# Matmuls and transposes kept in the order of the text, and the second product of the states laid in by pairs

## The chip, the cores and the metric

One NeuronCore of a Trainium2 chip runs the whole program. The metric is device time in microseconds. Three runs of the kernel before took 641.52, 642.74 and 642.97 us; the median is 642.74 us.

## What is computed

Two layers in a row, all in float32. The first is a cross attention between tokens and states, the second a mixture of experts that sends each row to one expert.

```python
# x: (8 batches, 8 heads, 512 tokens, 64), state: (8, 8, 32, 64)
a  = softmax(x @ state.T / 8);  xread = a @ state        # 512 token rows of a batch
a2 = softmax(state @ x.T / 8);  sread = a2 @ x           # 32 state rows of a batch
x  = concat([xread, sread], axis=2) -> (8 * 544, 512)    # heads side by side
logits = x @ w_gate                                      # 8 experts
e = argmax(logits); g = softmax(logits)[e]
out = g * (relu(x @ w1[e]) @ w2[e])                      # w1: 512 x 1024, w2: 1024 x 512
```

## The kernel before, in words

**Attention.** For each batch `b` a generator `front(b)` transposes the tokens (`transpose_x`, L183, four groups of four 128x128 transposes into the PSUM tile `pt`, each group copied out by ACT before the next can use the one buffer that the tag "m" has), prepares the states (`prep_state`, L168: two transposes, two copies into `stT`, four small matmuls `pg`, copied to `gst`), and forms the scores `pc` (L189). The softmax over states and the one over tokens run on DVE, ACT and GpSimd. `back(b)` transposes the token softmax `a2` (L227), forms the state rows `pw` (L237), stores them to `st_dram`, and forms the tokens' logits `pl` (L254). The tag "s" (`pg`, `pw`, `pl`, `pr`) has one PSUM buffer too. `finish(b)` (L361) routes some batches: logits to one-hot rows on DVE (`route`), then counts per expert on PE (`pr`, L298).

**Tokens' experts.** In each batch the tokens are sent through one expert, that of most of the batch's tokens, whose number SP reads from `eb` before it loads the weights `w1t` and `w2t` (2 MB each, L323 and L327). `states_w1` forms `G` (`pG`, L408), `up` (L413) forms 8 tiles `hT` of two matmuls `ph` each, and `down` (L425) four tiles `py` of eight matmuls each, scaled and stored by ACT. `up` and `down` take an `insert` function, `piece`, which is called after every second of these 128x512 matmuls and there runs the next piece of other work.

**States' experts.** During the first `up` and the batches 0 and 1 that other work is the attention of batches 2 to 7. Then `logits_s` (L262) reads all state rows back (`srow`), the last batches are routed, and the rows are grouped by expert: `prs` (L492) ranks them, DVE works out slots, GpSimd scatters the rows to `ss_dram`, and SP reads groups of four times 32 rows back as `xg` (L552). From there the other work is `rounds()` (L623): four rounds of `round_x` (transposes `ptx`), four steps of the first product `round_up` (`pgh`, L581: 8 matmuls of 32 columns each, from two tiles `s1`), `round_h` (relu, eight transposes `pth`), and eight steps of the second product `round_down` (`pgy`, L599: four matmuls of 32 columns from a tile `s2`). Each matmul of a group of four goes to another quarter of PE's columns, with another expert's weights. A tile `s1` or `s2` is 1 MB in four transfers that SP issues; there are 4 buffers of `s1` and 3 of `s2`, and `fetch` orders the next tile when one has been used. A `yield` ends a piece: three per step of the first product, two per step of the second.

**What sets the order.** A scheduler puts the instructions of each engine in order, by its own picture of time; on PE it may set a later matmul ahead of an earlier one. SP, ACT, DVE and GpSimd each run their own list in its order.

```python
            for f in range(NFC):
                round_down(r, f)
                fetch(0, 1)
                yield
                yield
```

The line numbers are those of the kernel before.

Of the kernel before, what the change touches and what calls it, by code (L numbers as in the profile page):

```python
# [20 lines left out]
def kernel(  # L21
# [146 lines left out]
    def prep_state(b):  # L168
        pt = ps_m.tile([128, 2, 2, 2, NS], FP32, tag="m", name="pt")
        for g in range(2):  # L170
            nc.tensor.transpose(pt[:, g], st2[:, 2 * b + g], ident[:])
        for i in range(2):

            evict(stT[ts(i, 64), b].rearrange("p (g j) n -> p g j n", g=2)[:, :, :, ts(i, NS)],
                  pt[ts(i, 64), :, :, i, :])

        pg = ps_s.tile([128, 2, E], FP32, tag="s", name="pg")
        for j in range(NPR):
            nc.tensor.matmul(pg[ds(64 * (j % 2), 64), j // 2, :], lhsT=stT[:, b, j, :], rhs=wg[:, j, :],
                             start=True, stop=True, skip_group_check=True)  # L180
        evict(gst[:, b], pg[:])

    def transpose_x(b, xT, j):  # L183
        pt = ps_m.tile([128, NC, 128], FP32, tag="m", name="pt")
        for c in range(NC):
            nc.tensor.transpose(pt[:, c, :], x_nat[b][:, c, ts(j, 2), :], ident[:])  # L186
        nc.scalar.copy(xT[:, j], pt[:])  # L187

    def scores(b, xT):  # L189

        pc = ps_c.tile([128, 2, S], FP32, tag="c", name="pc")
        for j in range(NPR):
            nc.tensor.matmul(pc[ts(j % 2, 64), j // 2, :], lhsT=stT[:, b, j, :], rhs=xT[:, j],  # L193
                             start=True, stop=True, skip_group_check=True)
        return pc

# [30 lines left out]
    def transpose_write(a2):  # L227

        a2T = att.tile([128, 2, NC, 128], FP32, tag="a2T", name="a2T")
        for g in range(2):  # L230
            pt = ps_m.tile([128, NC, 128], FP32, tag="m", name="pt")
            for c in range(NC):
                nc.tensor.transpose(pt[:, c, :], a2[:, g, ts(c, 128)], ident[:])  # L233
            nc.scalar.copy(a2T[:, g], pt[:])  # L234
        return a2T

    def write_rows(b, a2T, s2):  # L237


        pw = ps_s.tile([128, 2, 2, D], FP32, tag="s", name="pw")  # L240
        for g in range(2):
            for c in range(NC):
                for i in range(2):
                    nc.tensor.matmul(pw[ts(i, 64), g], lhsT=a2T[:, g, c, ts(i, 64)],  # L244
                                     rhs=x_nat[b][:, c, ts(2 * g + i, 2), :],
                                     start=(c == 0), stop=(c == NC - 1), skip_group_check=True)
        xs = att.tile([128, 2, 2, D], FP32, tag="xs", name="xs")
        for g in range(2):
            nc.vector.tensor_scalar(xs[:, g], pw[:, g], s2[:, g:g + 1], None, ALU.mult)
        for i in range(4):  # L250
            nc.scalar.dma_start(out=st_dram[ts(b, NS)].rearrange("n (g i d) -> n g i d", g=2, i=4)[:, :, i, :],
                                in_=xs[ts(i, NS), :, i % 2, :])

    def logits_x(b):  # L254
        pl = ps_s.tile([128, NC, E], FP32, tag="s", name="pl")
        for c in range(NC):
            for g in range(2):
                nc.tensor.matmul(pl[:, c, :], lhsT=aT[:, b, g, ts(c, 128)], rhs=gst[:, b, g, :],  # L258
                                 start=(g == 0), stop=(g == 1), skip_group_check=True)
        evict(lg[:, ts(b, NC)], pl[:])  # L260

    def logits_s():  # L262
        sT = att.tile([128, NST, NDC, 128], FP32, tag="sT", bufs=1, name="sT")
        pl = ps_s.tile([128, NST, E], FP32, tag="s", name="pls")
        for t in range(NST):
            nc.sync.dma_start(out=srow[:, t, 0:DM], in_=st_dram[ts(t, 128)])
            pt = ps_m.tile([128, NDC, 128], FP32, tag="m", name="pt")
            for c in range(NDC):
                nc.tensor.transpose(pt[:, c, :], srow[:, t, ts(c, 128)], ident[:])
            evict(sT[:, t], pt[:])  # L270
        for t in range(NST):
            for c in range(NDC):
                nc.tensor.matmul(pl[:, t, :], lhsT=sT[:, t, c, :], rhs=wg[:, c, :],
                                 start=(c == 0), stop=(c == NDC - 1), skip_group_check=True)
        evict(lg[:, NX:], pl[:])

# [21 lines left out]
    def choose(b0, nb):  # L298

        pr = ps_s.tile([128, nb, E], FP32, tag="s", name="pr")  # L300
        ohb = oh[:, 0:NX].rearrange("p (b c) e -> p b c e", c=NC)
        for c in range(NC):
            nc.tensor.matmul(pr[:], lhsT=ones_b[:], rhs=ohb[:, ds(b0, nb), c, :],
                             start=(c == 0), stop=(c == NC - 1), skip_group_check=True)
# [95 lines left out]
    def states_w1(w1t, st):  # L400

        G = ffn.tile([128, 2, F], FP32, tag="G", bufs=1, name="G")
        for g in range(2):
            for k in range(2):
                pg = ps_h.tile([128, 512], FP32, tag="h", name="pG")
                for i in range(2):
                    j = 2 * g + i
                    nc.tensor.matmul(pg[ts(i, 64), :], lhsT=st[:, j, :], rhs=w1t[:, j, ts(k, 512)],  # L408
                                     start=True, stop=True, skip_group_check=True)
                evict(G[:, g, ts(k, 512)], pg[:])  # L410
        return G

    def up(G, a, insert=None):  # L413
        hT = [ffn.tile([128, S], FP32, tag="hT", bufs=NFC, name="hT") for _ in range(NFC)]
        for f in range(NFC):
            ph = ps_h.tile([128, S], FP32, tag="h", name="ph")
            for g in range(2):
                nc.tensor.matmul(ph[:], lhsT=G[:, g, ts(f, 128)], rhs=a[:, g, :],  # L418
                                 start=(g == 0), stop=(g == 1))
            relu(hT[f][:], ph[:])  # L420
            if insert:
# [70 lines left out]
    pr = ps_s.tile([128, NST + 1, E], FP32, tag="s", name="prs")  # L492
    for t in range(NST):
        for u in range(t):
            nc.tensor.matmul(pr[:, t, :], lhsT=ones_b[:], rhs=oh[:, NX + u, :],
                             start=(u == 0), stop=False, skip_group_check=True)
        nc.tensor.matmul(pr[:, t, :], lhsT=U128[:], rhs=oh[:, NX + t, :],
                         start=(t == 0), stop=True, skip_group_check=True)
    for u in range(NST):
        nc.tensor.matmul(pr[:, NST, :], lhsT=ones_b[:], rhs=oh[:, NX + u, :],  # L500
                         start=(u == 0), stop=(u == NST - 1), skip_group_check=True)
    ng_i = const.tile([128, E], I32)
    nc.vector.tensor_scalar(ng_i[:], pr[:, NST, :], 31.0, None, ALU.add)
# [65 lines left out]
    def round_x(r):  # L569
        pt = ps_t.tile([128, NDC, 128], FP32, tag="t", name="ptx")  # L570
        for c in range(NDC):
            nc.tensor.transpose(pt[:, c, :], rd[r]["xg"][:, ts(c, 128)], ident[:])
# [5 lines left out]
    def round_up(r, k):  # L578
        for half in range(2):
            for q in range(4):  # L580
                nc.tensor.matmul(rd[r]["ph"][half][ts(q, 32), :], lhsT=rd[r]["xT"][:, k, ts(q, 32)],  # L581
                                 rhs=rd[r][1, k, half][:, q, :], start=(k == 0), stop=(k == NDC - 1),
                                 skip_group_check=True)

    def round_h(r):
# [4 lines left out]
        for u in range(2):  # L590
            pt = ps_t.tile([128, 4, 128], FP32, tag="t", name="pth")
            for i in range(4):
                nc.tensor.transpose(pt[:, i, :], h[:, ts(4 * u + i, 128)], ident[:])  # L593
            evict(hT[:, ts(u, 4)], pt[:])
        rd[r].update(hT=hT, py=ps_g.tile([128, DM], FP32, tag="g", bufs=2, name="pgy"))

    def round_down(r, f):
        for q in range(4):
            nc.tensor.matmul(rd[r]["py"][ts(q, 32), :], lhsT=rd[r]["hT"][:, f, ts(q, 32)],  # L599
                             rhs=rd[r][2, f][:, q, :], start=(f == 0), stop=(f == NFC - 1),  # L600
                             skip_group_check=True)

# [20 lines left out]
    def rounds():  # L623
# [3 lines left out]
        for r in range(NR):  # L627
# [128 lines left out]
```

## Time and profile before

| what | value |
|---|---|
| median of three runs | 642.74 us |
| the profiled execution's own time | 642.71 us |
| its span on the core | 640.8 us |
| PE busy | 600.3 us, 94% of the span |
| DVE, ACT, GpSimd busy | 131.6, 108.9, 23.4 us |
| moved by DMA | 123.15 MB, 192 GB/s over the span |
| `py` and `ph` matmuls, busy | 241.8 and 123.3 us |
| `pgh` and `pgy` matmuls, busy | 60.3 and 59.5 us |

A float32 matmul stands in the trace as two rows, one per pass, so `py` with its 256 matmuls has 512 rows. "x4" in a timeline is four such rows. The busy time of PE counts a stretch once where rows overlap. The idle time before a row, with what ended it, stands in brackets.

### The profile page before, as it was taken

What the parts mean: (1) busy time and instruction counts of PE and PEld (TensorE: products, weight loads), DVE (VectorE), ACT (ScalarE), POOL (GpSimd) and SP (SyncE); (2) the same over time, 40 slices, a digit from 0 to 9 for tenths busy, and PEclk for the clock granted to TensorE, in tenths of its full rate; (3) what the DMA queues carried; (4) which work ended last, traced back from release to release, by engine and by line L of the source; (5) the groups of instructions that cost most, each with busy time, mean ns of one, the idle gap of its engine ahead of it and who ended that gap; (6) DMA issues with size and microseconds to landing.
All of it is one profiled execution on the core that took longest, in us unless ns stands there. A gap on an engine that the chain in (4) does not pass through costs nothing.

```text
span 640.8 us, 6269 instructions
## 1 busy us (share of the span) xinstructions
PE 600.3 (94%) x2225; PEld 235.7 (37%) x2225; DVE 131.6 (21%) x287; ACT 108.9 (17%) x202; POOL 23.4 (4%) x29
## 2 busy tenths in 40 slices
PE   1778699999999999799999999999999999999997
PEld 0355334555455544123223242332322322333343
DVE  1335521544643414000110011000110001000100
ACT  1332311323413212001111010100111001111100
POOL 1011010101101101000000000000000000000000
PEclk9996799999999999999999999999999999999999
DMA  9433930376131044976985879677697779635501
GB/s 242 86 70 79 383 134 1 102 234 186 31 137 37 20 167 133 297 258 198 348 324 164 298 258 316 227 266 262 228 360 249 263 241 313 212 133 165 197 17 50
DMA packets 96497, 123.15 MB, mean 192 GB/s; under 512 B 45775, under 2 KB 45775, under 8 KB 96464
## 3 DMA queue, kind: packets, MB, share of 16 engines
q1 hardware_dynamic: 83552, 110.65, 52.8%
q10 hardware_dynamic: 12432, 11.04, 5.2%
q0 software_dynamic: 480, 1.05, 0.4%
q8 instruction: 18, 0.29, 0.2%
q14 instruction: 15, 0.12, 0.1%
HBM read 111.69 MB, written 11.54 MB: 192 GB/s over the span
## 4 chain that ended last, share of the span: by engine, by line
PE 85%; issue 6%; ACT 4%; DMA 3%; DVE 2%; ACTq 1%; SPq 0%; POOL 0%; POOLq 0%
PE py L429 33%; PE ph L418 16%; PE pgh L581 9%; PE pgy L599 8%; PE pG L408 4%; PE pc L193 4%; PE pt L186 3%; PE pw L244 2%; PE pl L258 2%; PE pt L233 1%; DMA st<-in_state_dram 1%; ACT xT L187 1%; DMA ss_dram<-srow,slot_i 1%; ACT a L221 1%; PE pth L593 1%
## 5 line engine op out<-in xcount | busy, mean ns | idle before, releaser
L429 PE MATMUL py<-w2t,hT 128*128 128x512 f32 x512 | 241.8, 606 | 0.0
L429 PEld LDWEIGHTS py<-w2t,hT 128*128 128x128 f32 x512 | 89.9, 190 | 129.4 <-issue 128.3
L418 PE MATMUL ph<-aT,G 128*128 128x512 f32 x256 | 123.3, 609 | 0.0
L418 PEld LDWEIGHTS ph<-aT,G 128*128 128x128 f32 x256 | 44.3, 189 | 66.0 <-issue 64.1
L581 PE MATMUL pgh<-s,sxT 128*32 128x512 f32 x256 | 60.3, 602 | 0.0
L442 ACT ACTIVATE y<-py,gw 128x512 f32<-128x512 f32 x32 | 22.0, 687 | 224.2 <-PE py L429 200.6
L599 PE MATMUL pgy<-s,shT 128*32 128x512 f32 x256 | 59.5, 604 | 0.0
L398 DVE TENSOR_SCALAR hT<-ph 128x512 f32<-128x512 f32 x31 | 21.4, 691 | 173.1 <-PE ph L418 173.1
L186 PE MATMUL pt<-ident,x_nat 128*128 128x128 f32 x128 | 26.3, 333 | 20.7 <-ACT xT L187 12.1
L396 ACT ACTIVATE hT<-ph 128x512 f32<-128x512 f32 x33 | 19.7, 596 | 129.4 <-PE ph L418 126.0
L408 PE MATMUL pG<-w1t,stT 128*64 128x512 f32 x128 | 34.7, 613 | 0.0
L186 PEld LDWEIGHTS pt<-ident,x_nat 128*128 128x128 f32 x128 | 18.0, 167 | 37.8 <-ACT xT L187 15.9
L193 PE MATMUL pc<-xT,stT 128*64 128x512 f32 x64 | 28.5, 773 | 0.0
L187 ACT COPY xT<-pt 128x512 f32<-128x512 f32 x32 | 18.7, 585 | 40.8 <-PE pt L186 40.8
L581 PEld LDWEIGHTS pgh<-s,sxT 128*32 128x32 f32 x256 | 9.4, 108 | 42.0 <-issue 32.8
L210 POOL TENSOR_TENSOR sx<-sx,sm 128x1024 f32<-128x1024 f32 x8 | 15.3, 1912 | 200.1 <-DVE sm L209 119.1
L599 PEld LDWEIGHTS pgy<-s,shT 128*32 128x32 f32 x256 | 8.6, 108 | 37.7 <-issue 33.1
L244 PE MATMUL pw<-x_nat,a2T 128*64 128x128 f32 x256 | 19.9, 304 | 0.0
L244 PEld LDWEIGHTS pw<-x_nat,a2T 128*64 128x64 f32 x256 | 17.1, 153 | 4.9 <-issue 4.4
L258 PEld LDWEIGHTS pl<-gst,aT 128*128 128x128 f32 x128 | 15.2, 194 | 5.8 <-issue 5.3
L607 POOL DMA_INDIRECT out_dram<-ys,xg x4 | 3.9, 977 | 361.7 <-DMA s<-in_moe_w_dram 202.0
L233 PE MATMUL pt<-ident,a 128*128 128x128 f32 x64 | 12.0, 319 | 4.2 <-ACT a2T L234 2.0
(117 smaller groups left out, 251.7 us busy)
## 6 DMA issues: line engine op xcount, KB each, us to landing
s<-in_moe_w_dram SPq DMA_DIRECT2D x256, 256.0 KB, 5.1
w1t<-in_moe_w_dram SPq DMA_DIRECT2D x8, 2048.0 KB, 8.0
w2t<-in_moe_w_dram SPq DMA_DIRECT2D x8, 2048.0 KB, 12.4
x_nat<-in_x_dram SPq DMA_DIRECT2D x32, 256.0 KB, 3.8
out_dram<-y ACTq DMA_DIRECT2D x32, 256.0 KB, 4.2
ss_dram<-blank ACTq DMA_DIRECT2D x4, 257.0 KB, 7.8
xg<-ss_dram SPq DMA_DIRECT2D x4, 257.0 KB
st<-in_state_dram ACTq DMA_DIRECT2D x2, 448.0 KB, 9.0
```

Source lines behind the costliest of these rows:

```text
L186: nc.tensor.transpose(pt[:, c, :], x_nat[b][:, c, ts(j, 2), :], ident[:])
L187: nc.scalar.copy(xT[:, j], pt[:])
L193: nc.tensor.matmul(pc[ts(j % 2, 64), j // 2, :], lhsT=stT[:, b, j, :], rhs=xT[:, j], start=True, stop=True, skip_group_check=True)
L244: nc.tensor.matmul(pw[ts(i, 64), g], lhsT=a2T[:, g, c, ts(i, 64)], rhs=x_nat[b][:, c, ts(2 * g + i, 2), :], start=(c == 0), stop=(c == NC ...
L258: nc.tensor.matmul(pl[:, c, :], lhsT=aT[:, b, g, ts(c, 128)], rhs=gst[:, b, g, :], start=(g == 0), stop=(g == 1), skip_group_check=True)
L398: nc.vector.tensor_scalar(dst, src, 0.0, None, ALU.max)
L408: nc.tensor.matmul(pg[ts(i, 64), :], lhsT=st[:, j, :], rhs=w1t[:, j, ts(k, 512)], start=True, stop=True, skip_group_check=True)
L418: nc.tensor.matmul(ph[:], lhsT=G[:, g, ts(f, 128)], rhs=a[:, g, :], start=(g == 0), stop=(g == 1))
L429: nc.tensor.matmul(py[:], lhsT=hT[f][:, ts(c, 128)], rhs=w2t[:, f, :], start=(f == 0), stop=(f == NFC - 1))
L442: nc.scalar.activation(y[:], py[:], AF.Copy, scale=gw[:, NC * b + c, :])
L581: nc.tensor.matmul(rd[r]["ph"][half][ts(q, 32), :], lhsT=rd[r]["xT"][:, k, ts(q, 32)], rhs=rd[r][1, k, half][:, q, :], start=(k == 0), sto ...
L599: nc.tensor.matmul(rd[r]["py"][ts(q, 32), :], lhsT=rd[r]["hT"][:, f, ts(q, 32)], rhs=rd[r][2, f][:, q, :], start=(f == 0), stop=(f == NFC ...
```

## The change

Every matmul and every transpose now goes through `mm` or `tp`, which tell the scheduler to leave PE's instructions in the order in which the text issues them. The second product of the states is laid in by two steps at a time: two steps, then four yields, in place of one step and two yields, twice.

```diff
+    def mm(*args, **kw):
+
+        tc.keep_in_program_order(nc.tensor.matmul(*args, **kw))
+
+    def tp(*args):
+        tc.keep_in_program_order(nc.tensor.transpose(*args))
+
...
-            nc.tensor.transpose(pt[:, g], st2[:, 2 * b + g], ident[:])
+            tp(pt[:, g], st2[:, 2 * b + g], ident[:])
...
-                nc.tensor.matmul(py[:], lhsT=hT[f][:, ts(c, 128)], rhs=w2t[:, f, :],
+                mm(py[:], lhsT=hT[f][:, ts(c, 128)], rhs=w2t[:, f, :],
...
-            for f in range(NFC):
-                round_down(r, f)
-                fetch(0, 1)
+            for f in range(0, NFC, 2):
+                for i in range(2):
+                    round_down(r, f + i)
+                    fetch(0, 1)
+                yield
+                yield
                 yield
                 yield
```

All other matmuls and transposes of the program are changed as the two shown. No instruction is added or taken away.

The rounds, on PE. `pgh` is the states' first product and `pgy` their second; the number in `s_1613` tells the weight tile. Before, near the start of round 0:

```order
L429 MATMUL py<-w2t,hT 128x512 x11
L572 MATMUL ptx<-ident,xg 128x128 x4
L429 MATMUL py<-w2t,hT 128x512
L581 MATMUL pgh<-s_1613,sxT 32x512 x2
L429 MATMUL py<-w2t,hT 128x512
L581 MATMUL pgh<-s_1613,sxT 32x512
L429 MATMUL py<-w2t,hT 128x512
L581 MATMUL pgh<-s_1613,sxT 32x512
L429 MATMUL py<-w2t,hT 128x512
L581 MATMUL pgh<-s_1618,sxT 32x512 x2
L429 MATMUL py<-w2t,hT 128x512
L581 MATMUL pgh<-s_1618,sxT 32x512
```

and now:

```order
L124 MATMUL py<-w2t,hT 128x512 x2
L127 MATMUL ptx<-ident,xg 128x128 x4
L124 MATMUL py<-w2t,hT 128x512 x4
L124 MATMUL pgh<-s_1613,sxT 32x512 x4
L124 MATMUL pgh<-s_1618,sxT 32x512 x4
L124 MATMUL py<-w2t,hT 128x512 x6
L124 MATMUL pgh<-s_1623,sxT 32x512 x4
L124 MATMUL pgh<-s_1628,sxT 32x512 x4
```

The eight matmuls of a step stand together, and from the first `ptx` on all 256 matmuls of 32 columns stand in 32 groups of eight, where before they stood in 101 groups of one to eleven. Nine `py` that stood ahead of the first `ptx` now stand behind it.

The end of routing, on PE: `srow` are state rows read back, `pls` their logits, `pr` the counts, `prs` the ranks. Before:

```order
L418 MATMUL ph<-aT,G 128x512 x2
L269 MATMUL pt<-ident,srow 128x128 x4
L418 MATMUL ph<-aT,G 128x512
L273 MATMUL pls<-wg,sT 128x8 x4
L418 MATMUL ph<-aT,G 128x512 x7
L269 MATMUL pt<-ident,srow 128x128 x4
L418 MATMUL ph<-aT,G 128x512
L273 MATMUL pls<-wg,sT 128x8 x4
L418 MATMUL ph<-aT,G 128x512 x3
L303 LDWEIGHTS ones_b
L303 MATMUL pr<-oh,ones_b 128x24
```

and now:

```order
L124 MATMUL ph<-aT,G 128x512 x2
L127 MATMUL pt<-ident,srow 128x128 x8
L124 MATMUL pls<-wg,sT 128x8 x8
L124 LDWEIGHTS ones_b
L124 MATMUL pr<-oh,ones_b 128x24
```

Both sets of row transposes, all of `pls` and `pr` now stand in one piece behind two of the `ph`; the other fourteen `ph` come behind `pr`, and `prs` behind those.

The attention of batches 3 and 2 inside `down`, on PE. `a_692` is the token softmax of one batch. Before:

```order
L186 MATMUL pt<-ident,x_nat 128x128 x4
L429 MATMUL py<-w2t,hT 128x512
L233 MATMUL pt<-ident,a_692 128x128 x4
L429 MATMUL py<-w2t,hT 128x512
L233 MATMUL pt<-ident,a_692 128x128 x4
L429 MATMUL py<-w2t,hT 128x512
L171 MATMUL pt<-ident,st_130 128x128 x2
L429 MATMUL py<-w2t,hT 128x512
L179 MATMUL pg<-wg,stT 64x8 x4
L193 MATMUL pc<-xT,stT 64x512
L244 MATMUL pw<-x_nat,a2T 64x128 x16
```

and now:

```order
L127 MATMUL pt<-ident,x_nat 128x128 x4
L127 MATMUL pt<-ident,a_692 128x128 x8
L124 MATMUL py<-w2t,hT 128x512 x2
L127 MATMUL pt<-ident,st_130 128x128 x2
L124 MATMUL pg<-wg,stT 64x8 x4
L124 MATMUL pw<-x_nat,a2T 64x128 x16
L124 MATMUL py<-w2t,hT 128x512 x2
L124 MATMUL pc<-xT,stT 64x512 x4
```

Groups that share one PSUM buffer, between which a `py` stood before, now stand next to each other. The same holds for five batches. Ahead of all this, the scheduler had set the token transposes and scores of batches 2 and 3 before the first `pG`; they now stand behind it, inside `up` and `down`.

## Rows read from the trace of the kernel before

**Rows 1.** The page, part 1: busy time, share and instructions of each engine.

```profile
PE 600.3 (94%) x2225; PEld 235.7 (37%) x2225; DVE 131.6 (21%) x287; ACT 108.9 (17%) x202; POOL 23.4 (4%) x29
```

**Rows 2.** PE timeline, second round: start, duration (us), line, tiles, rows merged.

```profile
330.84 1.05 PE L599 MATMUL pgy<-s,shT 128*32 128x512 f32 x4
331.82 1.12 PE L429 MATMUL py<-w2t,hT 128*128 128x512 f32 x2
332.88 1.04 PE L599 MATMUL pgy<-s,shT 128*32 128x512 f32 x2
```

**Rows 3.** PE timeline, last round and the end.

```profile
556.68 1.92 PE L581 MATMUL pgh<-s,sxT 128*32 128x512 f32 x16
558.53 5.42 PE L429 MATMUL py<-w2t,hT 128*128 128x512 f32 x12
563.88 1.93 PE L581 MATMUL pgh<-s,sxT 128*32 128x512 f32 x16
...
614.46 22.58 PE L429 MATMUL py<-w2t,hT 128*128 128x512 f32 x52
```

**Rows 4.** PE timeline, first and last visit to the 32-column matmuls.

```profile
262.85 1.67 PE L581 MATMUL pgh<-s,sxT 128*32 128x512 f32 x4
...
613.47 1.07 PE L599 MATMUL pgy<-s,shT 128*32 128x512 f32 x8
```

**Rows 5.** PE timeline, from the end of routing to the first round.

```profile
226.32 1.88 PE L418 MATMUL ph<-aT,G 128*128 128x512 f32 x4
...
237.68 0.63 PE L269 MATMUL pt<-ident,srow 128*128 128x128 f32 x4 [1.09 <-DMA srow<-st_dram]
...
239.00 1.04 PE L273 MATMUL pls<-wg,sT 128*128 128x8 f32 x8
...
242.55 0.25 PE L303 MATMUL pr<-oh,ones_b 128*128 128x24 bf16 x4
...
244.53 0.19 PE L500 MATMUL prs<-oh,ones_b 128*128 128x8 bf16 x2
...
261.44 0.63 PE L572 MATMUL ptx<-ident,xg 128*128 128x128 f32 x4 [3.33 <-DMA s<-in_moe_w_dram]
```

**Rows 6.** Timeline of SP's issues, the same stretch.

```profile
227.55 0.35 SPq L266 DMA_DIRECT2D srow<-st_dram  x1
...
258.22 0.34 SPq L552 DMA_DIRECT2D xg<-ss_dram  x1
259.10 11.13 SPq L558 DMA_DIRECT2D s<-in_moe_w_dram  x16
270.62 11.84 SPq L565 DMA_DIRECT2D s<-in_moe_w_dram  x12
```

**Rows 7.** PE timeline, attention: groups that wait for a copy, and one that doesn't.

```profile
71.20 0.66 PE L186 MATMUL pt<-ident,x_nat 128*128 128x128 f32 x4 [0.68 <-ACT xT L187]
...
78.83 0.60 PE L179 MATMUL pg<-wg,stT 128*64 128x8 f32 x8 [0.67 <-ACT stT L128]
...
126.00 0.60 PE L186 MATMUL pt<-ident,x_nat 128*128 128x128 f32 x4
126.43 1.02 PE L429 MATMUL py<-w2t,hT 128*128 128x512 f32 x2
```

**Rows 8.** SP's issue of the first weights.

```profile
61.96 0.39 SPq L325 DMA_DIRECT2D w1t<-in_moe_w_dram  x1
```

**Rows 9.** The view of the tile `w1t`: its eight loads.

```profile
DMA to landing us min/median/max: 7.7/8.0/10.4
```

**Rows 10.** PE timeline, the first `up`.

```profile
86.17 14.00 PE L418 MATMUL ph<-aT,G 128*128 128x512 f32 x32
```

**Rows 11.** Stretches: busy time by engine, PEclk (granted clock), DMA share, GB/s.

```profile
48.00:52.00 4.00, 2.59 (x10) 1.80 (x11) 3.58 (x11) 1.30 (x3) 0.00 (x0) 0.51 0.02 4
...
261.40:637.10 375.70, 374.11 (x1146) 117.01 (x1146) 29.29 (x42) 37.54 (x61) 3.91 (x4) 1.00 0.70 237
460.00:480.00 20.00, 20.00 (x62) 5.88 (x54) 2.77 (x4) 2.36 (x4) 0.00 (x0) 1.00 0.96 325
```

More of the change, by code (lines that the diff above doesn't have):

```diff
@@ L178, in prep_state @@
         for j in range(NPR):
-            nc.tensor.matmul(pg[ds(64 * (j % 2), 64), j // 2, :], lhsT=stT[:, b, j, :], rhs=wg[:, j, :],
+            mm(pg[ds(64 * (j % 2), 64), j // 2, :], lhsT=stT[:, b, j, :], rhs=wg[:, j, :],
                              start=True, stop=True, skip_group_check=True)
@@ L185, in transpose_x @@
         for c in range(NC):
-            nc.tensor.transpose(pt[:, c, :], x_nat[b][:, c, ts(j, 2), :], ident[:])
+            tp(pt[:, c, :], x_nat[b][:, c, ts(j, 2), :], ident[:])
         nc.scalar.copy(xT[:, j], pt[:])
@@ L192, in scores @@
         for j in range(NPR):
-            nc.tensor.matmul(pc[ts(j % 2, 64), j // 2, :], lhsT=stT[:, b, j, :], rhs=xT[:, j],
+            mm(pc[ts(j % 2, 64), j // 2, :], lhsT=stT[:, b, j, :], rhs=xT[:, j],
                              start=True, stop=True, skip_group_check=True)
@@ L243, in write_rows @@
                 for i in range(2):
-                    nc.tensor.matmul(pw[ts(i, 64), g], lhsT=a2T[:, g, c, ts(i, 64)],
+                    mm(pw[ts(i, 64), g], lhsT=a2T[:, g, c, ts(i, 64)],
                                      rhs=x_nat[b][:, c, ts(2 * g + i, 2), :],
@@ L257, in logits_x @@
             for g in range(2):
-                nc.tensor.matmul(pl[:, c, :], lhsT=aT[:, b, g, ts(c, 128)], rhs=gst[:, b, g, :],
+                mm(pl[:, c, :], lhsT=aT[:, b, g, ts(c, 128)], rhs=gst[:, b, g, :],
                                  start=(g == 0), stop=(g == 1), skip_group_check=True)
@@ L268, in logits_s @@
             for c in range(NDC):
-                nc.tensor.transpose(pt[:, c, :], srow[:, t, ts(c, 128)], ident[:])
+                tp(pt[:, c, :], srow[:, t, ts(c, 128)], ident[:])
             evict(sT[:, t], pt[:])
@@ L272, in logits_s @@
             for c in range(NDC):
-                nc.tensor.matmul(pl[:, t, :], lhsT=sT[:, t, c, :], rhs=wg[:, c, :],
+                mm(pl[:, t, :], lhsT=sT[:, t, c, :], rhs=wg[:, c, :],
                                  start=(c == 0), stop=(c == NDC - 1), skip_group_check=True)
@@ L302, in choose @@
         for c in range(NC):
-            nc.tensor.matmul(pr[:], lhsT=ones_b[:], rhs=ohb[:, ds(b0, nb), c, :],
+            mm(pr[:], lhsT=ones_b[:], rhs=ohb[:, ds(b0, nb), c, :],
                              start=(c == 0), stop=(c == NC - 1), skip_group_check=True)
@@ L407, in states_w1 @@
                     j = 2 * g + i
-                    nc.tensor.matmul(pg[ts(i, 64), :], lhsT=st[:, j, :], rhs=w1t[:, j, ts(k, 512)],
+                    mm(pg[ts(i, 64), :], lhsT=st[:, j, :], rhs=w1t[:, j, ts(k, 512)],
                                      start=True, stop=True, skip_group_check=True)
@@ L417, in up @@
             for g in range(2):
-                nc.tensor.matmul(ph[:], lhsT=G[:, g, ts(f, 128)], rhs=a[:, g, :],
+                mm(ph[:], lhsT=G[:, g, ts(f, 128)], rhs=a[:, g, :],
                                  start=(g == 0), stop=(g == 1))
@@ L494 @@
         for u in range(t):
-            nc.tensor.matmul(pr[:, t, :], lhsT=ones_b[:], rhs=oh[:, NX + u, :],
+            mm(pr[:, t, :], lhsT=ones_b[:], rhs=oh[:, NX + u, :],
                              start=(u == 0), stop=False, skip_group_check=True)
-        nc.tensor.matmul(pr[:, t, :], lhsT=U128[:], rhs=oh[:, NX + t, :],
+        mm(pr[:, t, :], lhsT=U128[:], rhs=oh[:, NX + t, :],
                          start=(t == 0), stop=True, skip_group_check=True)
     for u in range(NST):
-        nc.tensor.matmul(pr[:, NST, :], lhsT=ones_b[:], rhs=oh[:, NX + u, :],
+        mm(pr[:, NST, :], lhsT=ones_b[:], rhs=oh[:, NX + u, :],
                          start=(u == 0), stop=(u == NST - 1), skip_group_check=True)
@@ L580, in round_up @@
             for q in range(4):
-                nc.tensor.matmul(rd[r]["ph"][half][ts(q, 32), :], lhsT=rd[r]["xT"][:, k, ts(q, 32)],
+                mm(rd[r]["ph"][half][ts(q, 32), :], lhsT=rd[r]["xT"][:, k, ts(q, 32)],
                                  rhs=rd[r][1, k, half][:, q, :], start=(k == 0), stop=(k == NDC - 1),
@@ L598, in round_down @@
         for q in range(4):
-            nc.tensor.matmul(rd[r]["py"][ts(q, 32), :], lhsT=rd[r]["hT"][:, f, ts(q, 32)],
+            mm(rd[r]["py"][ts(q, 32), :], lhsT=rd[r]["hT"][:, f, ts(q, 32)],
                              rhs=rd[r][2, f][:, q, :], start=(f == 0), stop=(f == NFC - 1),
```

6 lines of the change are left out of this document (3 added, 3 removed).

## The prediction

> **What bounds the kernel now.** I read the busy times first. PE is busy for 600.3 of 640.8 us and no other engine for a quarter of that [rows 1], so the question is what PE's time is made of. Then I read PE's timeline in the rounds. A visit to the 32-column matmuls takes 0.98 us from its start to the next row's (330.84 to 331.82), whether it holds four rows or two: the one `py` behind it starts at 331.82, and the visit at 332.88 holds one matmul [rows 2]. That `py` takes 1.06 us (331.82 to 332.88), while in an unbroken run two rows take 0.87 us (22.58 us for 52 rows) [rows 3]. In the last round, where the same matmuls happen to stand in the order of the text, sixteen rows take 1.85 us (556.68 to 558.53), and the six `py` behind them 5.35 us (558.53 to 563.88) [rows 3]. So a group of four matmuls on four quarters of the columns costs as little as one alone, about 0.9 us, and each change between narrow and full matmuls costs some tenths. The reader is to see that PE's 94% hides matmuls that ran alone where four could have run together. Third, the places at which PE waits, since an order that may not be left turns waits into idle time: the end of routing [rows 5, 6], the attention [rows 7] and the first weights [rows 8 to 10].
>
> **The change part by part.** The sum is made against the profiled execution: 642.71 us, of which the span is 640.8, practically the median of 642.74.
>
> *1. The rounds, a gain.* Before, PE makes 101 visits to the 32-column matmuls; the first starts at 262.85, the last at 613.47 [rows 4]. From start to start of the next row they add up to 110.2 us. The new order has 32 visits of eight matmuls, at 1.85 us each [rows 3] 59.2 us: 51.0 us less. Behind a visit the first full matmuls pay 0.2 us (5.35 against 12 rows at 0.434, which is 5.21, gives 0.14; 1.06 against 0.87 gives 0.19); 69 visits fewer are 13 us less at 0.19. Against this, nine `py` that ran before the first `ptx` now come behind it: 9 x 0.87 = 7.8 us. The eight `pth` of a round now stand together though they share one PSUM buffer; each such pair of groups waits for the copy, some 0.9 us as worked out under 4, four times, 3.6 us, of which before paid about half: +2. Sum from the first `ptx` to the end of PE's work: -51 - 13 + 8 + 2 = **-54**. Bounds: if the visits cost 1.0 per four as in rows 2, 32 x 2.0 = 64, and -49; if nothing is paid for `pth`, -56.
>
> *2. The start of the rounds, a loss.* At `ptx` (261.44) SP has only begun: 16 transfers of `s1`, issued from 259.10 on for 11.13 us, then 12 of `s2` from 270.62 for 11.84 us [rows 6]. In the text's order step 3 of the first product comes about 19 us behind `ptx` (four `py` 3.5, then two visits of 1.85 and two runs of 5.35, and about 1 for the second tile). Its two tiles are transfers 29 to 36, queued on SP behind the other 28, which end at 282.46, 21 us behind `ptx`; eight more at the 0.7 us of the first sixteen are 5.6 us. That is 26.6, and PE would wait 7 or 8 us. It is less if the queue runs better without the pauses of the second group, so I take **+6**, from 0 to 12.
>
> *3. The end of routing, a loss.* Take as zero the end of batch 1's `down`, just before the `ph` at 226.32 [rows 5]. The second `srow` is issued right after, at 227.55 [rows 6], behind a 2 MB weight load, and is there at 237.68, 11.4 us on [rows 5]. Before, PE fills this with `ph`; now it has two of them, 1.7 us, and waits. From the transposes at 237.68 to `pr` at 242.55 are 4.9 us, which the text's order has to wait through too, and the other four `pls` (1.04 us at 239.00 [rows 5]) come in front: `pr` at 17.3. Then fourteen `ph` at 0.87, 12.2 us, part of them at the lower clock after such a wait (+2.5): `prs` at 32. From `prs` (244.53) to `ptx` (261.44) were 16.9 us [rows 5], through DVE, the scatter and `xg` (258.22 [rows 6]); PE has only the `pG` and two `py` for it. So `ptx` at 48.9, against 35.1 before: **+13.8**. Bounds: without the clock's part and with `pr` at once +10; +17 if the copies in between queue.
>
> *4. The attention, a loss.* Where two groups share a PSUM buffer, PE idles 0.68 us behind its 0.66 us of transposes [rows 7], 1.34 us where a group followed by a `py` takes 0.43 (126.00 to 126.43) [rows 7]: 0.9 us each. `pg` behind the state transposes idles 0.67 us the same way [rows 7]. In the new order each of five batches has four such neighbours (last token transposes and first `a2` transposes, the two halves of `a2`, state transposes and `pg`, `pg` and `pw`, which share the tag "s"), and two more stand alone: 22 waits, at 0.85 us **+18.7**. Bounds: 22 x 0.67 = 15; 25 if DVE or ACT are busy when the copy comes.
>
> *5. The front.* The token work of batches 2 and 3 no longer stands in front of the first `pG`. The first weights are issued at 61.96 [rows 8], once `pw` of batch 1 has let the fifth `x` load go. In the new order three groups of transposes leave the way to that `pw`, a `pr` enters it; I take 3 us earlier, 59, and 7.7 for landing [rows 9]: 66.7. Four pairs of `pG`, half of them at the lower clock, take some 6 us, so `up` starts near 73 in place of 86.17 [rows 10], -13. The moved work then costs, at the full clock, eight groups of token transposes at 0.43 (3.5), two of `a2` (0.9), states (1.2), and eight score matmuls, two side by side (16 rows x 0.217 + 2 x 0.2 = 3.9): +9.5. Sum **-3.5**, from -6 to +2 (weights not earlier at all, 61.96 + 8).
>
> *6. Transfers during the rounds.* The stretch from 261.4 on moved 237 GB/s over 375.7 us [rows 11], 89 MB. With part 1 the last visit ends some 295 us behind `ptx`, part 2 makes it 301: 296 GB/s have to flow. 20 us at 325 are in the trace [rows 11], so it can, but pairs of `s2` tiles out of three buffers have little slack. I take **+3**, from 0 to 20.
>
> The copies on ACT and DVE, the stores, GpSimd and DVE's softmax cost nothing: PE's matmuls cover them, as those engines are busy for a fifth of the span or less [rows 1].
>
> Sum: -54 + 6 + 13.8 + 18.7 - 3.5 + 3 = -16. 642.7 - 16 = 626.7, in round numbers **627 us**.
>
> **The rivals.**
>
> *The clock falls in the attention.* From 48 to 52 us the granted clock is 0.51, the lower of the two levels, 1.2 GHz [rows 11]; in that part of the program PE does transposes with waits between them, as at 71.20 [rows 7]. If each of the five batches of part 4 drops to that level for 10 us, the matmuls in it take 5 us more: 25 us, 652 us, slower. It turns the sign from 6.5 us of low clock per batch on. Against it: the stretch from 261.4 on keeps 1.00 [rows 11] although it comes right behind a wait of 3.33 us [rows 5], and part 4's waits are 0.7 us between full matmuls. The Trainium skill speaks for it, "TensorE: Matmul & The Clock Gate", section "HAM oscillation — how this bites in real kernels": bursts of matmuls with waits between them run throttled, every one of them. By that rule the time would be this rival's; the rows at 48 us bear it out, those behind 261.44 do not. Chance 0.08.
>
> *The transfers become the bound.* If the rounds' 89 MB flow at 265 GB/s, they take 336 us, 35 more than the 301, and the time is 627 - 3 + 35 = 659; at 280 it is 318 us and 641. So from 278 down the change is no gain. For it: each tile waits for a buffer, and two are now wanted at once. Against: the 325 over 20 us, with PE the slower side [rows 11]. Middle value 642; chance 0.12.
>
> *The waits of parts 2 to 4 are smaller.* If the start of the rounds costs 0, routing +10 and the attention +15, the time is 642.7 - 54 + 10 + 15 - 3.5 + 3 = 613. For it: what a wait delays is partly waited for again later (parts 2 and 3 overlap, as DMA goes on). Chance 0.17.
>
> **How the numbers follow.** The forecast, 627, has 0.63; its own range, from the bounds, is 615 to 639. The whole range has to leave out no more than 0.2: 606 takes in the third case, and 645 the better half of the transfers' case; the clock's case is left out. A measurement tells about 0.2%, 1.3 us, from no change. Faster by more: 0.61 of the forecast, all 0.17 of the third case and little of the transfers' case: 0.80. Same: 0.05. Slower: the clock, half of the transfers' case and a rest: 0.15.
>
> **What would show it.** Part 1 is right if the rounds show only visits of sixteen rows at 1.85 us, and the stretch from `ptx` to PE's end is near 327 us (375.6 before); wrong if 32-column rows wait for `s`. Part 2: a wait of several us at the third step of round 0. Part 3: PE idle for about 9 us before the second `srow` transposes and 11 before the first `ptx`. Part 4: idle time of 0.6 to 0.9 us in front of `a2` transposes, `pg` and `pw`, with the granted clock at 1.00 there. Part 5: the first `ph` near 73. The forecast falls if transfers hold PE in every round, or if the clock is low between 80 and 230 us.

## The result and the profile after

The changed kernel takes 625.38 us (median of 4 runs, 624.16 to 626.47) against 642.86 for the kernel before on the same chip: a ratio of 0.9728, with a 95% interval of 0.9701 to 0.9755. The forecast was 627. The profiled execution took 626.47 us, of which the span is 624.6; before it was 642.71 and 640.8, so the two profiles are 16.2 us apart.

The profiled execution of one experiment below (the text's order in the rounds alone) was disturbed, so that kernel was run once more for its profile.

The page's busy line of the kernel after, beside [rows 1]:

```profile
PE 541.8 (87%) x2225; PEld 241.4 (39%) x2225; DVE 132.1 (21%) x287; ACT 109.3 (17%) x202; POOL 23.4 (4%) x29
```

PE makes the same 2225 matmuls in 58.5 us less, but its share falls from 94% to 87%: the span fell by 16 us only, and the rest became idle time. The page's groups of the 32-column matmuls, first of the kernel after, then of before (tiles, count, busy us, mean ns, idle time before them):

```profile
L124 PE MATMUL pgh<-s,sxT 128*32 128x512 f32 x256 | 35.4, 620 | 6.7 <-DMA s<-in_moe_w_dram 6.7
L124 PE MATMUL pgy<-s,shT 128*32 128x512 f32 x256 | 31.7, 599 | 0.0
```

```profile
L581 PE MATMUL pgh<-s,sxT 128*32 128x512 f32 x256 | 60.3, 602 | 0.0
L599 PE MATMUL pgy<-s,shT 128*32 128x512 f32 x256 | 59.5, 604 | 0.0
```

The mean time of one is the same, about 0.6 us; what fell is their joint busy time, from 119.8 to 67.1 us, since four now run side by side. The reader sees here why a mean says nothing of matmuls that overlap.

PE's timeline of the kernel after at the stretch ends that the prediction used (start, duration, idle time before it):

```profile
72.83 1.98 PE L124 MATMUL ph<-aT,G 128*128 128x512 f32 x4
...
236.00 1.88 PE L124 MATMUL ph<-aT,G 128*128 128x512 f32 x4
...
247.34 1.09 PE L127 MATMUL pt<-ident,srow 128*128 128x128 f32 x4 [9.03 <-DMA srow<-st_dram]
...
253.51 0.28 PE L124 MATMUL pr<-oh,ones_b 128*128 128x24 bf16 x4 [1.86 <-DVE oh L297]
253.63 14.64 PE L124 MATMUL ph<-aT,G 128*128 128x512 f32 x28
...
283.62 1.09 PE L127 MATMUL ptx<-ident,xg 128*128 128x128 f32 x4 [9.43 <-DMA s<-in_moe_w_dram]
284.50 5.91 PE L124 MATMUL py<-w2t,hT 128*128 128x512 f32 x8
...
297.67 1.92 PE L124 MATMUL pgh<-s,sxT 128*32 128x512 f32 x16
299.52 5.42 PE L124 MATMUL py<-w2t,hT 128*128 128x512 f32 x12
311.62 6.46 PE L124 MATMUL pgh<-s,sxT 128*32 128x512 f32 x16 [6.68 <-DMA s<-in_moe_w_dram]
...
594.81 26.02 PE L124 MATMUL py<-w2t,hT 128*128 128x512 f32 x60
```

With the starts in [rows 3, 5, 10], and the end of PE's work at 594.81 + 26.02 = 620.83 (before 614.46 + 22.58 = 637.04), the difference falls into four stretches:

| stretch on PE | before, us | after, us | difference | forecast (parts) |
|---|---|---|---|---|
| to the first `ph` | 86.17 | 72.83 | -13.3 | -13 (5) |
| first `ph` to the end of batch 1's `down` | 140.15 | 163.17 | +23.0 | +28.2 (4, rest of 5) |
| from there to the first `ptx` | 35.12 | 47.62 | +12.5 | +13.8 (3) |
| first `ptx` to the end of PE's work | 375.60 | 337.21 | -38.4 | -45 (1, 2, 6) |
| sum | 637.04 | 620.83 | -16.2 | -16 |

The second stretch is the attention. PE's timeline of the kernel after in one batch, beside [rows 7]:

```profile
100.74 0.60 PE L127 MATMUL pt<-ident,x_nat 128*128 128x128 f32 x4
102.02 0.66 PE L127 MATMUL pt<-ident,a 128*128 128x128 f32 x4 [0.68 <-ACT xT L194]
103.35 0.66 PE L127 MATMUL pt<-ident,a 128*128 128x128 f32 x4 [0.68 <-ACT a2T L241]
103.84 1.88 PE L124 MATMUL py<-w2t,hT 128*128 128x512 f32 x4
105.56 0.38 PE L127 MATMUL pt<-ident,st 128*128 128x128 f32 x2
106.61 0.41 PE L124 MATMUL pg<-wg,stT 128*64 128x8 f32 x8 [0.67 <-ACT stT L135]
107.29 1.97 PE L124 MATMUL pw<-x_nat,a2T 128*64 128x128 f32 x32 [0.28 <-DVE gst L137]
```

All four forecast neighbours wait, three by 0.67 or 0.68 us and the last by 0.28. And the stretches of the kernel after, columns as in [rows 11]:

```profile
80.00:241.00 161.00, 143.89 (x755) 76.76 (x754) 66.82 (x132) 47.93 (x97) 11.47 (x6) 1.00 0.27 83
241.00:260.00 19.00, 10.80 (x34) 7.16 (x35) 3.58 (x20) 1.48 (x3) 0.00 (x0) 0.55 0.25 97
318.00:480.00 162.00, 160.54 (x593) 60.09 (x596) 17.41 (x25) 20.39 (x33) 1.96 (x2) 1.00 0.92 318
```

The clock stays at 1.00 through the whole attention, and falls to 0.55 around the 9 us wait for `srow`. In the rounds, once past the third step (from 318 us on), PE has next to no idle time while 318 GB/s flow.

### The profile page after: what moved, and what is told of

The parts are those of the page before. It is cut to its first block, busy times and chain, and to the rows that moved or that the text cites. A ratio compares the mean times of both kernels' runs of the same rounds, so it can differ in the third digit from the quotient of the medians.

```text
span 624.6 us, 6270 instructions
## 1 busy us (share of the span) xinstructions
PE 541.8 (87%) x2225; PEld 241.4 (39%) x2225; DVE 132.1 (21%) x287; ACT 109.3 (17%) x202; POOL 23.4 (4%) x29
## 4 chain that ended last, share of the span: by engine, by line
PE 77%; issue 8%; DMA 7%; ACT 4%; DVE 2%; SPq 1%; ACTq 1%; POOL 0%; POOLq 0%; DVEq 0%
PE py L124 34%; PE ph L124 16%; PE pgh L124 6%; PE pgy L124 5%; PE pt L127 5%; PE pG L124 4%; PE pw L124 3%; PE pc L124 2%; DMA w1t<-in_moe_w_dram 2%; PE pl L124 2%; DMA s<-in_moe_w_dram 1%; DMA ss_dram<-blank 1%; DMA ss_dram<-srow,slot_i 1%; ACT xT L194 1%; ACT a2T L241 1%
## 5 line engine op out<-in xcount | busy, mean ns | idle before, releaser
L124 PE MATMUL py<-w2t,hT 128*128 128x512 f32 x512 | 234.8, 604 | 0.0
L124 PEld LDWEIGHTS py<-w2t,hT 128*128 128x128 f32 x512 | 94.0, 192 | 119.7 <-issue 119.7
L124 PE MATMUL ph<-aT,G 128*128 128x512 f32 x256 | 119.4, 610 | 0.0
L124 PEld LDWEIGHTS ph<-aT,G 128*128 128x128 f32 x256 | 47.3, 194 | 59.7 <-issue 58.7
L124 PE MATMUL pgh<-s,sxT 128*32 128x512 f32 x256 | 35.4, 620 | 6.7 <-DMA s<-in_moe_w_dram 6.7
L127 PE MATMUL pt<-ident,x_nat 128*128 128x128 f32 x128 | 23.2, 306 | 18.3 <-ACT xT L194 9.5
L403 ACT ACTIVATE hT<-ph 128x512 f32<-128x512 f32 x33 | 19.7, 597 | 93.1 <-PE ph L124 93.1
L124 PE MATMUL pgy<-s,shT 128*32 128x512 f32 x256 | 31.7, 599 | 0.0
L194 ACT COPY xT<-pt 128x512 f32<-128x512 f32 x32 | 18.7, 584 | 32.4 <-PE pt L127 32.4
L124 PE MATMUL pl<-gst,aT 128*128 128x8 f32 x128 | 17.1, 270 | 6.0 <-DVE aT L218 6.0
L124 PEld LDWEIGHTS pG<-w1t,stT 128*64 128x64 f32 x128 | 7.8, 141 | 24.7 <-DVE G L137 7.6
L124 PE MATMUL pc<-xT,stT 128*64 128x512 f32 x64 | 17.3, 665 | 0.0
## 6 DMA issues: line engine op xcount, KB each, us to landing
w2t<-in_moe_w_dram SPq DMA_DIRECT2D x8, 2048.0 KB, 10.9
```

The source lines that it names most:

```text
L124: tc.keep_in_program_order(nc.tensor.matmul(*args, **kw))
L127: tc.keep_in_program_order(nc.tensor.transpose(*args))
L403: nc.scalar.activation(dst, src, AF.Relu)
```

## The experiments

Each ratio below is to the kernel before on the same chip. Its medians there were 642.1 to 644.0 us, so a difference between the times of two experiments can hold some 2 us that belong to the chips; differences between traces are given where they matter.

### One part of the change at a time

The text's order alone, with the second product laid in by single steps:

```diff
-            for f in range(0, NFC, 2):
-                for i in range(2):
-                    round_down(r, f + i)
-                    fetch(0, 1)
-                yield
-                yield
+            for f in range(NFC):
+                round_down(r, f)
+                fetch(0, 1)
                 yield
                 yield
```

> The order of the text kept, but the second product laid in by single steps as before. Theory (each visit to the 32-column matmuls has a fixed price of some tenths of a us): 32 visits of four at 1.0 us take the place of 16 of eight at 1.85 us, +2.4 us, and 16 more visits cost the full matmuls behind them 0.19 us each, +3.0: about 631 us against 625.4 of the change. Rival (the number of visits is not what pays, and single steps give the tiles of weights more slack): 625 us or less.

Measured: 631.25 us, ratio 0.9809 (0.9791 to 0.9826). The visits to `pgy` are now of eight rows, each 1.0 us from its start to the next row's:

```profile
330.60 1.07 PE L124 MATMUL pgy<-s,shT 128*32 128x512 f32 x8
331.60 3.70 PE L124 MATMUL ph<-aT,G 128*128 128x512 f32 x8
```

The two traces differ in the rounds. From the first `ptx` to the end of PE's work are 343.3 us here (279.54 to 600.26 + 22.58), and 337.2 in the kernel after: 6.1 more, where 5.4 were expected.

```profile
279.54 1.09 PE L127 MATMUL ptx<-ident,xg 128*128 128x128 f32 x4 [9.28 <-DMA s<-in_moe_w_dram]
...
600.26 22.58 PE L124 MATMUL py<-w2t,hT 128*128 128x512 f32 x52
```

The pairs alone, in the kernel before, whose order the scheduler sets:

```diff
-            for f in range(NFC):
-                round_down(r, f)
-                fetch(0, 1)
+            for f in range(0, NFC, 2):
+                for i in range(2):
+                    round_down(r, f + i)
+                    fetch(0, 1)
+                yield
+                yield
                 yield
                 yield
```

> The second product laid in by pairs, but the scheduler free to reorder. Theory (the gain is the kept order, since the scheduler takes the groups of four apart): 636 to 645 us, with visits of one matmul still in the trace. Rival (two steps at a time are what brings the gain): 625 to 632 us.

Measured: 640.69 us, ratio 0.9949 (0.9932 to 0.9967). The timeline of this kernel shows why it gains so little:

```profile
331.57 1.05 PE L599 MATMUL pgy<-s,shT 128*32 128x512 f32 x4
332.55 1.12 PE L429 MATMUL py<-w2t,hT 128*128 128x512 f32 x2
333.61 1.05 PE L599 MATMUL pgy<-s,shT 128*32 128x512 f32 x2
```

The scheduler takes the pair apart again, as in [rows 2]: 95 visits are left of 101. So the order is what lets four matmuls run side by side. The pairs save more under it than alone: 5.9 us by the times (631.25 to 625.38) and 6.1 in the rounds by the traces, against 3.3 by the times and 1.1 in the rounds (374.5 us from `ptx` to the end of PE's work, 375.6 before). By the intervals of the ratios the size of that difference stays open.

### Where the order helps and where it costs

The text's order in the rounds alone; ahead of them the scheduler orders as before.

```diff
+    keep = [False]
...
-        tc.keep_in_program_order(nc.tensor.matmul(*args, **kw))
+        d = nc.tensor.matmul(*args, **kw)
+        if keep[0]:
+            tc.keep_in_program_order(d)
...
     work = rounds()
+    keep[0] = True
```

> The order of the text kept only from the first round on; attention and routing ordered by the scheduler as in the kernel before. Theory (the kept order gains in the rounds alone and loses ahead of them): the first ptx comes at 261.4 us as before in place of 283.6, and from there the 337 us of the change: a span of about 602, a time of 602 to 606 us. Rival (the losses ahead are repaid later, since the rounds wait for transfers and not for PE): 615 us or more.

Measured: 605.63 us, ratio 0.9406 (0.9389 to 0.9423): 19.8 us less than the full change. The attention and the end of routing do give back what parts 3 to 5 had put there (+29.0 in the forecast, 13.8 + 18.7 - 3.5; +22.2 in the table). Its profile, by a second run:

> The kernel with the text's order in the rounds alone, again, for its profile: 604 to 607 us. Part 4 and 3 of the prediction expect no wait for srow of over 2 us, and transposes of the attention with py between them. If the transfers set the pace of the rounds, waits for s of 5 us or more stand in its rounds; if only their start does, they stand at the first three steps alone.

Measured: 606.79 us. The waits of PE, by what it waited for (us in total, times, longest):

```profile
PE ptx L131 <- DMA s<-in_moe_w_dram: 10.7, 1, 10.7
PE pgh L126 <- DMA s<-in_moe_w_dram: 7.9, 1, 7.9
PE pt L131 <- DMA srow<-st_dram: 1.2, 1, 1.2
```

The `srow` wait is 1.2 us here, and 9.0 in the kernel after: part 3. But the waits at `ptx` and at the third step are there too, so they come with the order in the rounds. The one at the third step is part 2. The one at `ptx` makes `ptx` no later than before (261.04 and 261.44): PE lacks there the nine `py` that now stand behind it, the +8 of part 1.

```profile
261.04 1.08 PE L131 MATMUL ptx<-ident,xg 128*128 128x128 f32 x4 [10.73 <-DMA s<-in_moe_w_dram]
```

So `ptx` comes 22.6 us earlier than in the kernel after (283.62), much as the table has it. The spans are only 19.7 us apart (604.9 and 624.6), because from `ptx` on this run takes 2.9 us longer. Tiles of `s` are waited for longer in it: 7.9 us in place of 6.7 at the third step, and more inside two visits.

### The start of the rounds

First guess: the third step waits because its `s1` tiles stand on SP behind twelve `s2` transfers [rows 6]. So `s1` went first, and `s2` after the second step:

```diff
-        fetch(S1B, S2B)
+        fetch(S1B, 0)
...
+                if r == 0 and k == 1:
+                    fetch(0, S2B)
```

> The change, with the first three tiles s2 ordered after the second step of round 0 in place of at its start, so that the tiles of step 3 are no longer queued behind them. Theory (the wait of 6.7 us before the third step and its slow matmuls are a matter of the order of the queue): that wait falls to 0 to 2 us, 614 to 619 us. Rival (the transfers' rate sets it, and the wait goes to the second product, whose tiles are now late): 623 to 627 us, with a wait before the first pgy.

Measured: 624.18 us, ratio 0.9698 (0.9678 to 0.9718). The guess fell and the rival held. The third step no longer waits, but the second half of a visit to `pgy` does, in PE's timeline:

```profile
338.78 3.76 PE L124 MATMUL pgy<-s,shT 128*32 128x512 f32 x8 [5.88 <-DMA s<-in_moe_w_dram]
```

One wait of 6.7 us became one of 5.9. What is short is not a tile's place in the queue but time: 50 us into the rounds the transfers still have not caught up, in either order, and the wait goes to the tile that comes last.

Second guess: give the transfers time by letting PE do full matmuls there. The kernel after ends with 60 rows of `py` behind the last visit, 26.02 us in which nothing else is left. Ten empty pieces move 40 of these rows ahead of the first `ptx`, behind the issue of the first tiles:

```diff
         fetch(S1B, S2B)
+        for _ in range(10):
+            yield
         for r in range(NR):
```

> The kernel after, with ten empty pieces between the issue of the first round's transfers and its first transposes, so that twenty full matmuls (17.4 us) run there that now run behind the last visit (60 rows there, 20 would be left). Theory (the start of the rounds is idle time only because PE's order leaves nothing to do while the queue fills; the transfers have slack later): the idle before ptx (9.4 us), the wait at the third step (6.7 us) and the low clock behind them (some 6 us) go, 601 to 608 us. Rival (the rounds' transfers as a whole set the end; a wait removed comes back at a later tile, as when s1 was put ahead of s2): 616 to 625 us, with waits for s of several us in later steps.

Measured: 609.02 us, ratio 0.9483 (0.9461 to 0.9505), just above the theory's 601 to 608 and far from the rival's. PE's timeline:

```profile
270.64 19.15 PE L124 MATMUL py<-w2t,hT 128*128 128x512 f32 x44
289.63 0.60 PE L127 MATMUL ptx<-ident,xg 128*128 128x128 f32 x4
...
309.11 5.75 PE L124 MATMUL pgh<-s,sxT 128*32 128x512 f32 x16 [1.04 <-DMA s<-in_moe_w_dram]
...
594.31 8.85 PE L124 MATMUL py<-w2t,hT 128*128 128x512 f32 x20
```

The 44 rows ahead of `ptx` are the 40 moved and the four that stood there before. No idle time is left before it, the wait at the third step falls from 6.68 to 1.04 us, and the end keeps 20 rows. The order had left PE without work at one place and with 17 us of spare work at another.

### The end of routing

Both `srow` loads are issued, ten `ph` follow, and only then come the transposes:

```diff
         for t in range(NST):
             nc.sync.dma_start(out=srow[:, t, 0:DM], in_=st_dram[ts(t, 128)])
+        for _ in range(5):
+            yield
+        for t in range(NST):
             pt = ps_m.tile([128, NDC, 128], FP32, tag="m", name="pt")
...
-            logits_s()
+            yield from logits_s()
...
-            finish(b)
+            yield from finish(b)
```

> The kernel after, with the end of routing in two pieces: both srow loads are issued, ten ph follow, and only then the transposes of srow, pls and pr; four ph are left ahead of prs. Theory of part 3 (the fixed order has PE wait for the second srow with the ph behind it, which delays prs and all behind it): the wait for srow (9.0 us) falls under 2 us, the ph run at the full clock, ptx comes 11 to 15 us earlier, 610 to 615 us. Rival (what is won there is waited for again at ptx or at the third step, since the transfers set the time): 620 to 626 us.

Measured: 614.55 us, ratio 0.9571 (0.9542 to 0.9600). PE's timeline:

```profile
233.02 10.46 PE L124 MATMUL ph<-aT,G 128*128 128x512 f32 x24
243.32 0.60 PE L127 MATMUL pt<-ident,srow 128*128 128x128 f32 x4
...
269.69 1.09 PE L127 MATMUL ptx<-ident,xg 128*128 128x128 f32 x4 [9.34 <-DMA xg<-ss_dram]
...
297.89 5.75 PE L124 MATMUL pgh<-s,sxT 128*32 128x512 f32 x16 [6.11 <-DMA s<-in_moe_w_dram]
```

The wait for `srow` is gone, and `ptx` stands 36.7 us behind the end of batch 1's `down` in place of 47.6: 10.9 us, all of which reach the end. The waits at `ptx` and at the third step stay as they were (9.34 and 6.11). So the end of routing and the start of the rounds are two separate losses. Both repairs together:

> The two runs before in one: text's order everywhere, end of routing in two pieces, ten empty pieces ahead of the first round's transposes. Theory: the two idle times are separate places, so their gains add up (10.8 and 16.4 us against 625.4): 596 to 601 us. Rival (transfers then hold the rounds): 604 to 609 us, with waits for s of several us.

Measured: 600.07 us, ratio 0.9342 (0.9324 to 0.9360). The sum of the two gains, 16.4 + 10.8, would be 598.2.

### The neighbours that share a buffer

On top of that, one full matmul between the neighbours of part 4. The attention's generators yield `"h"` where only one matmul is to follow, and `up` and `down` call in after every matmul:

```diff
     def piece():
-        next(work, None)
+        units[0] -= 1
+        if units[0] == 0:
+            units[0] = 1 if next(work, None) == "h" else 2
...
         for g in range(2):
+            yield "h"
             pt = ps_m.tile([128, NC, 128], FP32, tag="m", name="pt")
...
+        yield "h"
         pg = ps_s.tile([128, 2, E], FP32, tag="s", name="pg")
...
+        yield "h"
         write_rows(b, a2T, s2)
```

The same is done between the two `srow` transposes, and two `ph` go between `pls` and `pr`.

> As the run above, and one full matmul set between the neighbours that share a PSUM buffer: last token transposes, both halves of a2, state transposes and pg, pg and pw; paid for by giving the first token transposes one matmul behind them in place of two. Theory of part 4 (each such neighbour costs PE its wait for the copy): the waits for a2T, stT and gst of after go (6.1, 5.8 and 1.7 us of idle time, 14 to 17 us with the fill behind each), 581 to 587 us, under the 588.8 of the free order ahead of the rounds. Rival (another wait takes their place, for the softmax on DVE and ACT or at srow, since the attention has its own chain): a gain under 6 us, 591 us or more.

Measured: 581.06 us, ratio 0.9060 (0.9030 to 0.9090), 19.0 less than the run above. PE's timeline of a batch's end of softmax, of the two ends of the attention and of the first `ptx`:

```profile
69.04 1.98 PE L124 MATMUL ph<-aT,G 128*128 128x512 f32 x4
...
97.87 0.64 PE L127 MATMUL pt<-ident,a 128*128 128x128 f32 x4
98.34 1.02 PE L124 MATMUL py<-w2t,hT 128*128 128x512 f32 x2
99.20 0.63 PE L127 MATMUL pt<-ident,a 128*128 128x128 f32 x4
...
219.53 10.46 PE L124 MATMUL ph<-aT,G 128*128 128x512 f32 x24
...
259.63 0.60 PE L127 MATMUL ptx<-ident,xg 128*128 128x128 f32 x4
```

From the first `ph` to the end of batch 1's `down` are 150.5 us (69.04 to 219.53), against 163.2 in the kernel after (and, by its timeline, in the run above): 12.7 us. Between there and `ptx` it gains 4.1 more (40.1 against 44.2). The two profiled executions are 20.0 us apart; the rest is 1.1 us in the rounds and 2.1 of an earlier first `ph` (69.04 against 71.13). Those 2.1 need not be this edit's: in six kernels with the same instructions ahead of it (the kernel after and the five runs above that keep the text's order everywhere) the first `ph` starts between 68.34 and 72.83. The time is at the lower edge of the range expected, and the attention's part is slightly under the 14 to 17 expected.

### A free order ahead of the rounds, with full matmuls at their start

The order is kept in the rounds alone, as above, and the ten empty pieces are put in ahead of the first round's transposes.

> Free order ahead of the rounds, the text's order in them, and the ten empty pieces of the run above. Theory: the wait of 2.9 us before ptx goes, and the wait for tiles at the start, whose size isn't known, with it: 594 to 603 us. Rival (transfers set the time of the rounds): 604 to 607 us, nothing won against 605.6.

Measured: 588.78 us, ratio 0.9158 (0.9136 to 0.9180), better than the theory's range: the waits that went were 10.7 us before `ptx`, where the expectation had 2.9, and 7.9 at the third step, which it did not know. One wait for `s` of 1.6 us is left there. The version of the section before, with the text's order everywhere, is still 7.7 us faster, and it is the best of this study.

## Why the prediction was right

*Part 1, the rounds: held.* The visits are of sixteen rows at 1.85 us (297.67 to 299.52). From the start of each to the next row's, the 32 visits add up to 64.9 us, where 101 visits took 110.2; two of them hold waits (6.46 and 2.82 us long), and without these it is 59.5, forecast 59.2. Of the stretch's -38.4, the start of the rounds and one late tile account for +14.4, so part 1 as a whole is -53, forecast -54. The sign that the prediction named for it, a stretch near 327 us, did not come (337.2), mainly because that figure holds part 2 at +6. That it is the number of visits that costs is shown by the two single parts: order alone makes 48 visits and gains less, pairs alone leave 95 and gain 0.5%.

*Part 2, the start of the rounds: the step that was mis-sized.* "I take +6, from 0 to 12", and it was 13.5, outside its own bounds: 6.7 of waiting at the third step, as forecast (7 or 8), but then 2.3 us because the four `py` behind `ptx` ran at a low clock (5.91 us for eight rows at 0.59, 3.60 in the run with full matmuls there), and 4.5 in the visit itself (6.46 against 1.92; 5.75 of it stay at the full clock, in the runs with full matmuls ahead, and at 0.66, in the run with the order in the rounds alone, so the clock is not what makes it long). The working had given 7 or 8 for the wait and I took less; and I had reckoned the wait up to the step's first slice only. The others come one by one behind it; how that shows is told below. And I had counted the lower clock in part 3, but not behind the wait before `ptx`.

*Part 3, the end of routing: held.* +12.5, forecast +13.8. PE waits 9.03 us for the second `srow` (forecast about 9), 1.86 for `pr`, and 9.43 before `ptx` (forecast 11; with the order in the rounds alone it waits 10.73 there, so it is the late `prs`, and not this wait, that makes `ptx` late); the fourteen `ph` take 14.64 us with the clock's part, forecast 14.7. The run with the `ph` in front of the transposes took 10.9 us of it back.

*Part 4, the attention: the mechanism right, the price too high.* Between the first `ph` and the end of batch 1's `down` the view of waits counts exactly 22 waits for copies of `xT`, `a2T`, `stT` and `gst`, as forecast, with 13.4 us of idle time. Seventeen are of 0.67 to 0.89 us, most of them as [rows 7] had it; the five between `pg` and `pw` are 0.28, since `gst` is a small copy that I had priced as a large one. By the starts in the timeline a batch pays 0.83 + 0.83 + 0.79 + 0.34 = 2.8 us for its four neighbours, forecast 4 x 0.85 = 3.4; over five batches and the two single ones that is 15.6 in place of 18.7. The other 2 us by which the stretch fell short of its forecast lie in the moved work of part 5, in the score matmuls `pc`. From start to start they take 11.2 us in this stretch, 48 rows, in place of 9.7 for 34: +1.5 for 14 rows, where +3.9 was forecast for 16. Before, rows of `pw` stood among them; now they stand together.

*Part 5, the front: held, so closely by luck.* First weights issued at 57.70, forecast 59; first `pG` at 67.54, forecast 66.7; first `ph` at 72.83, forecast 73. The six kernels named above have it between 68.34 and 72.83.

*Part 6, transfers: held, a little better than forecast.* Behind the third step only one visit is longer than 1.92 us by more than a few tenths (2.82 at 351.88): +1, forecast +3.

So 627 came out because two errors met: part 2 with the rounds 6.6 us too good, the attention with part 3 6.5 too bad. The mechanisms held; that the sum came within 2 us of the measured time is luck.

*The rivals.* The clock rival falls: 1.00 from 80 to 241 us, where it wanted 0.5 in every batch. The Trainium skill, "TensorE: Matmul & The Clock Gate", section "HAM oscillation — how this bites in real kernels", tells of bursts of matmuls that are shorter than the waits between them. Part 4's waits of 0.7 us between full matmuls are not that case, so the prediction had stretched the page too far; behind the wait of 9 us for `srow` the trace agrees with it (0.55 from 241 to 260). The transfers' rival falls: in the kernel after all visits behind the third step but one take 1.92 or 1.93 us while 318 GB/s flow, so PE waits for no tile in most of the rounds. In the best version, 17 us of whose full matmuls were moved ahead of this stretch, PE shows as busy for 311.6 of the 315.8 us from `ptx` on:

```profile
259.60:575.40 315.80, 311.59 (x1125) 115.33 (x1123) 29.29 (x42) 36.84 (x59) 3.92 (x4) 1.00 0.80 276
```

But that busy time counts waits inside a visit as work, as told below. Five of its 32 visits are longer than 1.85 us, by 9.8 us together (5.4 in the kernel after), so there the transfers cost some 10 us at single tiles and do not set the time of the rounds. The third rival, smaller waits, was half true of part 4 and wrong of part 2, where the wait did not shrink.

## What to carry to other kernels

An order that may not be left is worth what the scheduler's order breaks up, here four narrow matmuls that run side by side only as neighbours, and costs every wait that the scheduler had filled; price the two apart, stretch by stretch, and look where spare full matmuls stand that could fill the waits. Having fixed the order, write it as a schedule: with one matmul between neighbours that share a buffer, a late load's cover in front of it and the spare `py` at the start of the rounds, the same matmuls took 581 us instead of 625. And a wait that moves to the next tile when a queue is reordered is a shortage of time, to be met with other work and not with another order of the queue.

## What the hardware showed that I had not expected

A visit's own row can hide waits. In the best version the third visit takes 5.75 us on PE at a clock of 1.00, without idle time inside the row. The weight loads of the same stretch (engine PEld, same columns) show what PE does there:

```profile
278.70 0.14 PEld L124 LDWEIGHTS pgh<-s,sxT 128*32 128x32 f32 x2 [1.46 <-DMA s<-in_moe_w_dram]
279.38 0.14 PEld L124 LDWEIGHTS pgh<-s,sxT 128*32 128x32 f32 x2 [0.54 <-DMA s<-in_moe_w_dram]
```

There are eight of them, the first waiting 1.46 us for its slice of `s` and the others 0.43 to 0.62, one slice about every 0.68 us. So in that visit the transfers set the pace and the four matmuls run one after the other; PE's busy time counts them as work, and the view of waits shows only the first wait. Of two visits to `pgy` later on, of 4.1 and 4.6 us from their start (408.17 and 477.31) to the next row's, it shows 0.5 us in all. In the second of them:

```profile
478.87 0.14 PEld L124 LDWEIGHTS pgy<-s,shT 128*32 128x32 f32 x2 [1.41 <-DMA s<-in_moe_w_dram]
479.54 0.14 PEld L124 LDWEIGHTS pgy<-s,shT 128*32 128x32 f32 x2 [0.53 <-DMA s<-in_moe_w_dram]
```

The length of a visit tells such a wait, where PE's share of busy time does not.

The clock also fell without a long wait. In the run with both repairs, transposes and `pls` with waits of 0.68 and 1.85 us between them fill 245.9 to 250.4, and the `ph` behind them ran at 0.69:

```profile
245.90:250.40 4.50, 2.65 (x25) 2.48 (x25) 2.33 (x9) 0.47 (x2) 0.00 (x0) 0.96 0.00 0
250.40:255.40 5.00, 5.00 (x12) 2.12 (x10) 2.18 (x12) 0.00 (x0) 0.00 (x0) 0.69 0.00 0
```

With full matmuls between the same steps the granted clock stayed at 1.00 there (229 to 242 us of that run), which is part of the 4.1 us gained. What exactly lowers it was not tried apart.
